# Attention forward from chunk 1 on in exponentials of 1536 columns, with two score banks of three and the background work re-timed

## The chip, the cores and the metric

One core of a Trainium2 chip runs the whole kernel: TensorE (PE) with its weight loads (PEld), VectorE (DVE), ScalarE (ACT), GpSimd (POOL), SyncE (SP, whose queue issues DMAs) and 16 DMA engines. The metric is device microseconds of one execution, the median over the runs of a kernel. PSUM, where matmuls write, has eight banks of 512 float32 columns on 128 partitions; the sizes below are counted in these banks.

## The reference

One transformer block with adaptive layer norm, forward and backward. With S = 2048 tokens, D = 512, H = 32 heads of 16, F = 1792:

```python
h = _layernorm(x) * (1 + ca) + sa
q, k, v = split_heads(h @ wqkv)
o = softmax(q @ k.T / 4) @ v
x = x + ga * (o @ wo)
h = _layernorm(x) * (1 + cb) + sb
x = x + gb * (relu(h @ w1 + b1) ** 2 @ w2 + b2)
# outputs: x, and the gradients of A_x, wqkv, wo, w1, b1, w2, b2, c, w_mod for grad_out
```

The attention of the forward pass has 32 heads x 2048 x 2048 scores, and each of them goes through one exponential on ScalarE. The backward pass computes scores and exponentials once more; the change does not touch that part.

## The kernel before, in words

Tokens are cut into four chunks of 512 queries (`SC` = 4). The forward pass runs attention chunk by chunk, and while chunk c is in attention, the matmuls of the MLP of chunk c-1, forward and backward, are slipped between its matmuls.

**Chunk 0** has its own loop in `phase_fwd` (exponential at L413), with the projections as its background. **Chunks 1 to 3** run in `fwd_rest`, which the change rewrites. Its work is 24 groups: 3 chunks x 8 groups of 4 heads. A group walks 16 key blocks of 128 keys (`kb`). One step of that loop:

- four score matmuls (L503), one per head, each on 32 rows of the PE array and 512 queries, into two tiles of two PSUM banks. The pool `fwst` has three such tiles, six banks
- two exponentials of 1024 columns on ACT (L507), PSUM to bf16 tiles `pu` in SBUF (`fwp`, six buffers)
- the "pv" matmuls of the step before (L482): for each head four matmuls of 17 columns (16 of V and a column of ones that gives the softmax sum), 16 in a step, all 4 heads x 4 query blocks of a group accumulating in 272 columns of one bank, `accbank`
- up to four matmuls of the background (`bg.burst(3.0, self, most)`), nearly all of them recorded at L158, the line of the helper `mm`
- for each of the `most` slots that the background left free, a filler matmul of 512 columns (L520) into the score tile of the next step, which the real scores overwrite later

At a group's last step DVE takes the reciprocal of the sums and multiplies (L488, L490) before `accbank` is used again; `pend` holds pv back for a step there (`held`).

The background is a queue of generators (`Background`). `burst` adds `rate` to a credit (at most 4), takes matmuls while there is credit and fewer than `most` were taken, and stops behind the last matmul of an accumulation (`k.stopped`), since the background has one PSUM bank (`mps`, one buffer) that DVE must empty first. A yielded `("wait", n)` sets `hold` to n, and each later call of `burst` then only lowers `hold`, by 2 in before, until it is no longer positive.

`gen_mlp(sc, O_b)` yields in this order: the output projection (16 matmuls), for chunk 0 the folding of bias and scales into the weights (`gen_weights_1`: 14 times four matmuls of one column, then POOL scales w1 in four pieces, L1238), a wait, the first MLP product (56 matmuls, `pps<-fT,w`), for chunk 0 `gen_weights_2`, the gradient du (56), the gradient dx (4 x 14, each followed by layer-norm backward on DVE) with `gen_do` (4 x 4) between, and the output product fc2 (4 x 15). The mark `fc2_{sc}` is yielded after `fc2(0)`; once `fc2_2` has been seen in chunk 3, the loop takes no more background, and what is left goes to `last_chunk`, which runs the MLP of chunk 3 without attention beside it: `bg.take` puts some of the left matmuls between its own, and `bg.drain` emits the rest ahead of the transposes of the normalized activations (`turn(xh[...])`, L882).

PE and SP run in the order written in the program in this phase; instructions of ACT, DVE and POOL are placed by the framework's scheduler. Waits on buffers and on data come from the framework. The rest of the kernel (weight gradients, attention backward, L1076 on) is the same in both kernels.

Of the kernel before, what the change touches and what calls it, by code (L numbers as in the profile page):

```python
# [9 lines left out]
BF16 = mybir.dt.bfloat16  # L10
F32 = mybir.dt.float32
ACT = mybir.ActivationFunctionType
ALU = mybir.AluOpType
AX = mybir.AxisListType
PSUM = bass.MemoryType.PSUM
# [4 lines left out]
P = 128  # L20
DH = 16
# [14 lines left out]
class Background:  # L36
# [41 lines left out]
    def burst(self, rate, k, most=4):  # L78

        n = 0  # L80
        if self.hold > 0:
            self.hold -= 2
            return n
        self.credit = min(self.credit + rate, 4.0)
        while self.gens and self.credit > 0 and n < most:
            k.stopped = False
            r = self.next()
            if r is None:
                break
            if isinstance(r, tuple):  # L90
                self.hold = r[1]
                break
            self.credit -= max(r, 0.25)
            n += r
            if k.stopped:
                break
        return n
# [29 lines left out]
class K:  # L127
# [164 lines left out]
    def phase_fwd(self):  # L292
# [5 lines left out]
        tc, nc, pp = self.tc, self.nc, self.pp  # L298
        S, D, H, NQ, ST, DT, FT, SC = self.S, self.D, self.H, self.NQ, self.ST, self.DT, self.FT, self.SC
# [15 lines left out]
        Vaug = fw.tile([P, ST, H, DH + 1], BF16, name="Vaug")  # L315
        kp = self.open_pool("fwk", bufs=2)
        pup = self.open_pool("fwp", bufs=6)
        self.mps = self.open_pool("mps", bufs=2, space=PSUM)
        stp = self.open_pool("fwst", bufs=2, space=PSUM)
        accp = self.open_pool("fwacc", bufs=2, space=PSUM)  # L320
        O32 = self.ra.tile([P, 4, D], F32, name="O32")
        QTm = [fw.tile([P, 512], BF16, name=f"QTm{j}") for j in range(4)]
# [16 lines left out]
        bg = Background()  # L339
        bg.add(self.gen_qkv(kp))  # L340
        pend = []
# [18 lines left out]
        KT = kp.tile([P, S], BF16, name="KTq")  # L360
# [8 lines left out]
        for n in range(2):  # L369
            accb = accp.tile([P, 512], F32, name="accbank")  # L370
            accs.append(accb[:, 0:8 * (DH + 1)].rearrange("p (a s e) -> p a s e", a=2, s=4))
        units = [(n, 4 * s + k) for s in range(SC) for n in range(2) for k in range(4)]
        for i, (n, kb) in enumerate(units):
# [4 lines left out]
            for a in range(2):  # L378
                nc.tensor.matmul(stt[:, a, :], lhsT=KT[:, kb * P:(kb + 1) * P], rhs=(QTm[2 + a] if n else QTo[a])[:],
                                 start=True, stop=True)  # L380
# [58 lines left out]
        self.fwd_rest(bg, KT, kp, pup, QTm, Vaug, O32)  # L439
        bg.until(f"fc2_{SC - 2}")  # L440
        self.OT_l = self.mk.tile([P, 4, DT, P], BF16, name="fT", bufs=2)
        self.gT_l = self.mk.tile([P, DT, 512], BF16, name="fT", bufs=2)
        nc.sync.dma_start_transpose(self.gT_l[:], self.io["grad_out"][0, S - 512:, :])
        x0s = []
        for k in range(2):
            t = self.mk.tile([P, D], BF16, name="x0", bufs=2)
# [15 lines left out]
    def fwd_rest(self, bg, KT, kp, pup, QTm, Vaug, O32):  # L462

        nc, NQ, ST, SC = self.nc, self.NQ, self.ST, self.SC
        for name in ("fwacc", "fwst", "mps"):
            self.close_pool(name)
        self.mps = self.open_pool("mps", bufs=1, space=PSUM)
        stp = self.open_pool("fwst", bufs=3, space=PSUM)
        accp = self.open_pool("fwacc", bufs=1, space=PSUM)
        groups = [(qc, g) for qc in range(1, SC) for g in range(NQ)]  # L470
        acc = None

        def pv(w):
            nonlocal acc
            ((qc, g, kb, pus), half) = w
            if kb == 0 and half == 0:
                accb = accp.tile([P, 512], F32, name="accbank")
                acc = accb[:, 0:16 * (DH + 1)].rearrange("p (a s e) -> p a s e", a=4, s=4)
            for a in range(2):
                j = 2 * half + a  # L480
                for sub in range(4):
                    nc.tensor.matmul(acc[:, j, sub, :], lhsT=pus[half][:, a, sub * P:(sub + 1) * P], rhs=Vaug[:, kb, 4 * g + j, :],  # L482
                                     start=(kb == 0 and j == 0 and sub == 0), stop=False, skip_group_check=True)
            if kb < ST - 1 or half == 0:
                return
            st0 = 4 * qc
            rl = self.rl[:, st0:st0 + 4, 4 * g:4 * g + 4].rearrange("p s a -> p a s")
            nc.vector.reciprocal(rl, acc[:, :, :, DH])  # L488
            o = O32[:, :, 4 * g * DH:4 * (g + 1) * DH].rearrange("p s (a d) -> p a s d", a=4)
            nc.vector.tensor_tensor(o, acc[:, :, :, 0:DH], rl.unsqueeze(3).to_broadcast([P, 4, 4, DH]), ALU.mult)  # L490
            if g == NQ - 1 and qc < SC - 1:
                bg.add(self.gen_mlp(qc, self.take_o(qc, O32)))

        pend = []
        tiles = None
        for n, (qc, g) in enumerate(groups):
            for kb in range(ST):
                if kb == 1 and n + 1 < len(groups):
                    KTn = self.load_group_fwd(*groups[n + 1], kp, QTm)
                tiles = tiles or [stp.tile([P, 2, 512], F32, name="st") for _ in range(2)]  # L500
                for h in range(4):
                    r = slice(32 * h, 32 * h + 32)
                    nc.tensor.matmul(tiles[h // 2][:, h % 2, :], lhsT=KT[r, kb * P:(kb + 1) * P], rhs=QTm[g % 2][r, :],  # L503
                                     start=True, stop=True)
                pus = [pup.tile([P, 2, 512], BF16, name="pu") for _ in range(2)]
                for t, pu in zip(tiles, pus):
                    nc.scalar.activation(pu[:], t[:], ACT.Exp, scale=self.scale)  # L507
                held = kb == 1 and n > 0
                while len(pend) > 1 and not held:
                    pv(pend.pop(0))  # L510
                most = 5 if held else 2 if kb == 2 and n > 0 else 4
                done = 0 if qc == SC - 1 and f"fc2_{SC - 2}" in bg.seen else bg.burst(3.0, self, most)
                if pend and not held:
                    pv(pend.pop(0))
                pend += [((qc, g, kb, pus), half) for half in range(2)]
                tiles = None
                if (n, kb) != (len(groups) - 1, ST - 1):
                    tiles = [stp.tile([P, 2, 512], F32, name="st") for _ in range(2)]
                    for _ in range(int(most - done)):
                        nc.tensor.matmul(tiles[0][:, 0, :], lhsT=KT[:, 0:P], rhs=QTm[g % 2][:], start=True, stop=True)  # L520
            KT = KTn
        while pend:
            pv(pend.pop(0))

    def gen_open(self, Vaug, KT, QTm, QTo, stp, bg):

# [695 lines left out]
    def gen_weights_1(self):  # L1222

        nc = self.nc
        D, F, DT, FT = self.D, self.F, self.DT, self.FT
        w1, wo = self.w1, self.wo
        pb = self.mps.tile([P, 1024], BF16, name="pps")
        nc.tensor.transpose(pb[:, :FT], self.b1r[:], self.ident[:FT, :FT])
        nc.vector.tensor_copy(self.b1c_b[:], pb[:, :FT])
        pt = self.mps.tile([P, 512], F32, name="pps")  # L1230
        for ft in range(FT):
            for kt in range(DT):
                self.mm(pt[:, ft:ft + 1], lhsT=w1[:, kt, ft * P:(ft + 1) * P], rhs=self.sbT_b[:, kt:kt + 1],
                                 start=(kt == 0), stop=(kt == DT - 1))
            yield 0.5
        nc.vector.tensor_tensor(self.bias1[:], pt[:, :FT], self.b1c_b[:], ALU.add)
        for kt in range(DT):
            nc.gpsimd.tensor_scalar(w1[:, kt, :], w1[:, kt, :], self.opcbT[:, kt:kt + 1], 1.0, ALU.mult, ALU.mult)  # L1238
            yield 0
        nc.sync.dma_start_transpose(self.wogaT[:].rearrange("p a b c -> p (a b) c"), wo[:].rearrange("p a b -> p (a b)"))  # L1240
# [28 lines left out]
    def gen_mlp(self, sc, O_b):  # L1269
# [33 lines left out]
        nc.gpsimd.dma_start(tm_v(self.xhat2_d), xh[:])  # L1303
        if sc == 0:
            yield from self.gen_weights_1()
            yield ("wait", 4)
        else:
            yield ("wait", 11)
        rT = self.ra.tile([P, FT * 512], BF16, name="rT")[:].rearrange("p (f k) -> p f k", f=FT)
# [18 lines left out]
            nc.vector.tensor_tensor(rT[:, ft, :], rT[:, ft, :], rT[:, ft, :], ALU.mult)  # L1328
        nc.gpsimd.dma_start(self.duT_d.rearrange("ft p s -> p ft s")[:, :, s0:s0 + 512], duT[:])
        nc.gpsimd.dma_start(self.aT_d.rearrange("ft p s -> p ft s")[:, :, s0:s0 + 512], rT[:])  # L1330
        yield ("wait", 1)
        todo = []
        for k in range(4):
# [20 lines left out]
        def fc2(k):  # L1354
            pt = mps.tile([P, 512], F32, name="pps")
            for ft in range(FT):
                self.mm(pt[:], lhsT=rT[:, ft, k * P:(k + 1) * P], rhs=self.w2[:, ft, :], start=(ft == 0), stop=False)
                yield 1
            self.mm(pt[:], lhsT=self.ones_b[0:1, :], rhs=self.b2gb_b[0:1, :], start=False, stop=True)
            yield 1  # L1360
            o = mk.tile([P, D], BF16, name="o0", bufs=2)
            nc.vector.tensor_tensor(o[:], pt[:], x1[:, k, :], ALU.add)
            nc.gpsimd.dma_start(out_v[:, k, :], o[:])

        yield from fc2(0)
        yield from self.gen_do(sc, *todo.pop(0))
        yield (f"fc2_{sc}", 0)
        for k in range(1, 4):
            yield from fc2(k)

    def ln_bwd_dve(self, wk, dxh_ps, xh, g, rstd_col, out_ap):
        nc = self.nc
# [695 lines left out]
```

## Time and profile before

| what | us |
|---|---|
| runs (median of 3) | 2517.16 (2512.57 to 2521.45) |
| the profiled execution, as timed | 2527.3 |
| its span in the trace | 2525.3 |
| chunk 0 and what comes ahead of it | 0 to about 273 |
| `fwd_rest`, first to last exponential (L507) | 275.1 to 984.3 |
| `last_chunk`, the MLP of chunk 3 | about 984 to 1062 |

The time of the profiled execution is some 10 us over the median of the runs. In the rows, "x768 | 704.9, 1127 | 6.0" is the count, then the time in which at least one instruction of the group was running, the mean duration of one in ns (neighbours overlap, so count times mean is more than the busy time), and the idle time of that engine just ahead of them. A matmul of 512 columns has a recorded duration of some 380 ns with its way through the array, while the next one starts much earlier. PEclk is the clock granted to TensorE, as a share of full speed.

### The profile page before, as it was taken

What the parts mean: (1) busy time and instruction counts of PE and PEld (TensorE: products, weight loads), DVE (VectorE), ACT (ScalarE), POOL (GpSimd) and SP (SyncE); (2) the same over time, 40 slices, a digit from 0 to 9 for tenths busy, and PEclk for the clock granted to TensorE, in tenths of its full rate; (3) what the DMA queues carried; (4) which work ended last, traced back from release to release, by engine and by line L of the source; (5) the groups of instructions that cost most, each with busy time, mean ns of one, the idle gap of its engine ahead of it and who ended that gap; (6) DMA issues with size and microseconds to landing.
All of it is one profiled execution on the core that took longest, in us unless ns stands there. A gap on an engine that the chain in (4) does not pass through costs nothing.

```text
span 2525.3 us, 69141 instructions
## 1 busy us (share of the span) xinstructions
PE 2424.0 (96%) x26994; PEld 1032.7 (41%) x27199; DVE 1683.0 (67%) x3343; ACT 2283.0 (90%) x3757; POOL 715.7 (28%) x1265
## 2 busy tenths in 40 slices
PE   8999999999999999989999999999999999999988
PEld 4555444545554544573232333332333333333333
DVE  6222212322342333576999999999999999999857
ACT  7999999999999996533999999999999999999934
POOL 2344430120121021246222332322332323222323
PEclk9999999999999999999999999999999999999999
DMA  4689650451244054599999999999999999999997
GB/s 166 133 179 209 162 124 22 127 118 48 99 103 100 22 145 120 111 188 214 236 237 226 233 237 232 236 226 228 230 233 234 233 234 234 239 227 238 241 179 188
DMA packets 1291630, 454.19 MB, mean 180 GB/s; under 512 B 1235796, under 2 KB 1260246, under 8 KB 1291302
## 3 DMA queue, kind: packets, MB, share of 16 engines
q1 hardware_dynamic: 1252422, 344.68, 72.4%
q0 software_dynamic: 36800, 104.04, 14.1%
q8 instruction: 212, 3.47, 0.6%
q10 hardware_dynamic: 2080, 1.05, 0.2%
q14 instruction: 116, 0.95, 0.1%
HBM read 75.83 MB, written 64.49 MB: 56 GB/s over the span
## 4 chain that ended last, share of the span: by engine, by line
PE 40%; ACT 8%; DMA 8%; issue 2%; DVE 2%; POOL 0%; SPq 0%; DVEq 0%; ACTq 0%; POOLq 0%
PE st L1710 16%; PE acckv L1561 8%; ACT pu L1713 6%; PE accq L1586 5%; DMA dsT<-ds 4%; PE dps L1151 2%; PE dp L1624 2%; DMA keep<-ds 1%; DMA dqT<-dq_t 1%; ACT csq L1642 1%; PE st L1856 1%; DVE ds L1628 1%; PE dp L1761 1%; PE st L1667 1%; PE st L1574 1%
## 5 line engine op out<-in xcount | busy, mean ns | idle before, releaser
L1628 DVE TENSOR_TENSOR ds<-dp,pu 128x512 bf16<-128x512 f32 x1888 | 1166.8, 684 | 36.5 <-PE dp L1624 20.6
L1713 ACT ACTIVATE pu<-st 128x512 bf16<-128x512 f32 x2048 | 1073.6, 666 | 37.2 <-PE st L1710 21.3
L507 ACT ACTIVATE pu<-st 128x1024 bf16<-128x1024 f32 x768 | 704.9, 1127 | 6.0 <-PE st L503 5.6
L1624 PE MATMUL dp<-kvm,q 64*128 64x512 bf16 x1024 | 364.0, 383 | 2.1 <-DVE ds L1628 1.0
L1624 PE MATMUL dp<-kvm,dOTg 64*128 64x512 bf16 x1024 | 364.9, 384 | 1.0 <-DVE ds L1628 0.8
L1710 PE MATMUL st<-kvm,QTg 64*128 64x512 bf16 x1024 | 348.8, 382 | 6.0
L1710 PE MATMUL st<-kvm,q 64*128 64x512 bf16 x1024 | 347.9, 381 | 5.1 <-ACT pu L1713 0.2
L1643 POOL TENSOR_TENSOR ds<-csq,pu 128x512 bf16<-128x512 f32 x128 | 147.2, 1150 | 626.5 <-ACT csq L1642 547.4
L482 PEld LDWEIGHTS <-pu 128*128 128x128 bf16 x6144 | 216.5, 96 | 158.0 <-issue 83.2
L482 PE MATMUL accbank<-Vaug,pu 128*128 128x17 bf16 x6144 | 265.2, 172 | 10.1 <-ACT pu L507 7.4
L520 PE MATMUL st<-QTm,KTq 128*128 128x512 bf16 x670 | 202.7, 379 | 6.3 <-ACT pu L507 2.7
L413 ACT ACTIVATE pu<-st 128x1024 bf16<-128x1024 f32 x224 | 206.6, 1060 | 2.3 <-PE st L410 1.9
L503 PE MATMUL st<-QTm,KTq 32*128 32x512 bf16 x1536 | 171.9, 385 | 5.2 <-issue 1.0
L1561 PE MATMUL acckv<-ds,Qg 128*16 128x512 bf16 x1024 | 176.5, 383 | 0.2
L1561 PE MATMUL acckv<-pu,dOg 128*16 128x512 bf16 x1024 | 176.4, 383 | 0.0
L1561 PE MATMUL acckv<-ds,q 128*16 128x512 bf16 x1024 | 175.8, 382 | 0.0
L1561 PE MATMUL acckv<-pu,q 128*16 128x512 bf16 x1024 | 175.8, 382 | 0.0
L410 PE MATMUL st<-QTm,KTq 128*128 128x512 bf16 x435 | 130.0, 377 | 10.1 <-ACT pu L413 4.0
L1710 PEld LDWEIGHTS <-q 64*128 64x128 bf16 x1024 | 66.9, 94 | 162.9 <-issue 150.0
L1710 PEld LDWEIGHTS <-QTg 64*128 64x128 bf16 x1024 | 67.1, 94 | 161.5 <-issue 146.5
L347 PEld LDWEIGHTS <-pu 128*128 128x128 bf16 x2048 | 86.4, 96 | 59.6 <-issue 3.0
L1624 PEld LDWEIGHTS <-q 64*128 64x128 bf16 x1024 | 88.8, 93 | 51.3 <-issue 40.8
(399 smaller groups left out, 3365.7 us busy)
## 6 DMA issues: line engine op xcount, KB each, us to landing
KTq<-KTq_d POOLq DMA_DIRECT2D x24, 512.0 KB, 3.8
duT_d<-auT POOLq DMA_DIRECT2D x3, 1792.0 KB, 7.3
aT_d<-rT POOLq DMA_DIRECT2D x3, 1792.0 KB, 11.9
KTq_d<-KTq SPq DMA_DIRECT2D x32, 128.0 KB, 2.2
QTq_d<-ev_fm SPq DMA_DIRECT2D x32, 128.0 KB, 4.4
ktm_d<-ev_tm POOLq DMA_DIRECT2D x32, 128.0 KB, 2.6
VTq_d<-vT POOLq DMA_DIRECT2D x4, 1024.0 KB, 6.1
dx<-dx_d SPq DMA_DIRECT2D x16, 256.0 KB, 4.6
```

The source lines that it names most:

```text
L410: nc.tensor.matmul(stt[:, a, :], lhsT=KT[:, kb * P:(kb + 1) * P], rhs=QTm[2 * jp + a][:], start=True, stop=True)
L413: nc.scalar.activation(pu[:], stt[:], ACT.Exp, scale=self.scale)
L482: nc.tensor.matmul(acc[:, j, sub, :], lhsT=pus[half][:, a, sub * P:(sub + 1) * P], rhs=Vaug[:, kb, 4 * g + j, :], start=(kb == 0 and j == ...
L503: nc.tensor.matmul(tiles[h // 2][:, h % 2, :], lhsT=KT[r, kb * P:(kb + 1) * P], rhs=QTm[g % 2][r, :], start=True, stop=True)
L507: nc.scalar.activation(pu[:], t[:], ACT.Exp, scale=self.scale)
L520: nc.tensor.matmul(tiles[0][:, 0, :], lhsT=KT[:, 0:P], rhs=QTm[g % 2][:], start=True, stop=True)
L1561: nc.tensor.matmul(acckv[r:r + DH, :], lhsT=T[n][:, ib, col:col + DH], rhs=src[:, a, :], start=(ib == 0), stop=(ib == ST - 1))
L1624: nc.tensor.matmul(dp[:], lhsT=T["dOT"][rd, ib * P:(ib + 1) * P], rhs=masked["VT"][a][rd, 512 * c:512 * (c + 1)], start=True, stop=True)
L1628: nc.vector.tensor_tensor(dsg[:, i, a], dp[:], pu[:, a, :], ALU.mult)
L1643: nc.gpsimd.tensor_tensor(dsg[:, i, 1], f[:], pu[:, 1, :], ALU.mult)
L1710: nc.tensor.matmul(stt[:], lhsT=T["QT"][rs, q], rhs=masked["KT"][a][rs, c0:c0 + 512], start=True, stop=True)
L1713: nc.scalar.activation(pu[:, a, :], stt[:], ACT.Exp, scale=self.scale)
```

## The change

- `fwd_rest` no longer goes by key blocks with four heads but by **units of three score tiles**: the 24 x 16 x 4 = 1536 tiles (group, key block, head) are cut into 512 units of three. A unit has three score matmuls into one tile of three banks (`fwst`: two tiles of three banks in place of three of two) and one exponential of 1536 columns. `pu` has four buffers of 1536 columns; `fwp` is closed and opened anew for that.
- pv works per tile (four matmuls of 17 columns): `outputs` takes up to six tiles that are at least two units old; the first call in a unit, ahead of the scores, only where a group's last tile is among them. Behind a group's end it holds the next group's tiles for one or two units.
- The background gets at most `int((1.32 - spent) / 0.215)` matmuls in a unit and a rate of 2.5, where `spent` is 0.33 for the scores and 0.1 for each pv tile. `hold` falls by 1.4 in a call.
- Fillers: while an accumulator is open, matmuls of 240 columns into the unused columns 272 to 511 of `accbank`; between accumulators, the unit's own scores repeated.
- `gen_weights_1` waits (2) ahead of its matmuls and yields 1 for each four; the wait behind it goes from 4 to 10.
- The turned grad_out of chunk 3 (`gT_l`, a transposing DMA on SP's queue) is asked for inside the MLP of chunk 2, ahead of dx, in place of after the loop.
- The mark `fc2_{sc}` comes after `fc2(1)` in place of `fc2(0)`.

```diff
@@ burst
-            self.hold -= 2
+            self.hold -= 1.4
@@ phase_fwd
         self.OT_l = self.mk.tile([P, 4, DT, P], BF16, name="fT", bufs=2)
-        self.gT_l = self.mk.tile([P, DT, 512], BF16, name="fT", bufs=2)
-        nc.sync.dma_start_transpose(self.gT_l[:], self.io["grad_out"][0, S - 512:, :])
@@ fwd_rest
-        stp = self.open_pool("fwst", bufs=3, space=PSUM)
+        stp = self.open_pool("fwst", bufs=2, space=PSUM)
         accp = self.open_pool("fwacc", bufs=1, space=PSUM)
+        pup = self.open_pool("fwp", bufs=4)
...
+        tiles = [(n, kb, h) for n in range(len(groups)) for kb in range(ST) for h in range(4)]
+        units = [tiles[i:i + 3] for i in range(0, len(tiles), 3)]
+        pend, ready = [], 0
+
+        def outputs(u, last_of):
+            nonlocal ready
+            n = 0
+            while n < 6 and pend and pend[0][0] <= u - 2 and not (accb is None and u < ready):
+                if last_of and not any(t[1:] == (ST - 1, 3) for (v, t, _) in pend if v <= u - 2):
+                    break
+                (_, t, p) = pend.pop(0)
+                n += 1
+                if pv(*t, p):
+                    ready = u + (1 if bg.hold > 0 or not bg.gens else 2)
+            return n
+
+        for u in range(len(units) + 2):
+            spent = 0.1 * outputs(u, True)
+            if u < len(units):
+                st = stp.tile([P, 3, 512], F32, name="st")
+
+                def scores():
+                    for i, (n, kb, h) in enumerate(units[u]):
+                        r = slice(32 * h, 32 * h + 32)
+                        nc.tensor.matmul(st[:, i, :], lhsT=KTs[n][r, kb * P:(kb + 1) * P], rhs=QTm[n % 2][r, :],
+                                         start=True, stop=True)
+
+                for (n, kb, h) in units[u]:
+                    if (kb, h) == (1, 0) and n + 1 < len(groups):
+                        KTs[n + 1] = self.load_group_fwd(*groups[n + 1], kp, QTm)
+                scores()
+                spent += 0.33
+            spent += 0.1 * outputs(u, False)
+            if u >= len(units):
+                continue
+            if groups[n][0] < SC - 1 or f"fc2_{SC - 2}" not in bg.seen:
+                spent += 0.215 * bg.burst(2.5, self, int((1.32 - spent) / 0.215))
+            if accb is not None:
+                for _ in range(int((1.2 - spent) / 0.1)):
+                    nc.tensor.matmul(accb[:, W:512], lhsT=KTs[n][:, 0:P], rhs=QTm[n % 2][:, W:512], start=False, stop=False,
+                                     skip_group_check=True)
+            else:
+                for _ in range(int((1.1 - spent) / 0.33)):
+                    scores()
+            pu = pup.tile([P, 3, 512], BF16, name="pu")
+            nc.scalar.activation(pu[:], st[:], ACT.Exp, scale=self.scale)
+            pend += [(u, t, pu[:, i, :]) for i, t in enumerate(units[u])]
@@ gen_weights_1
+        yield ("wait", 2)
...
-            yield 0.5
+            yield 1
@@ gen_mlp
-            yield ("wait", 4)
+            yield ("wait", 10)
...
+        if sc == SC - 2:
+            self.gT_l = mk.tile([P, DT, 512], BF16, name="fT", bufs=2)
+            nc.sync.dma_start_transpose(self.gT_l[:], io["grad_out"][0, self.S - 512:, :])
         yield ("wait", 1)
...
         yield from self.gen_do(sc, *todo.pop(0))
+        yield from fc2(1)
         yield (f"fc2_{sc}", 0)
-        for k in range(1, 4):
-            yield from fc2(k)
+        yield from fc2(2)
+        yield from fc2(3)
```

More of the change, by code (lines that the diff above doesn't have):

```diff
@@ L464, in fwd_rest, with pv @@
         nc, NQ, ST, SC = self.nc, self.NQ, self.ST, self.SC
-        for name in ("fwacc", "fwst", "mps"):
+        for name in ("fwacc", "fwst", "mps", "fwp"):
             self.close_pool(name)
         self.mps = self.open_pool("mps", bufs=1, space=PSUM)
-        stp = self.open_pool("fwst", bufs=3, space=PSUM)
+        stp = self.open_pool("fwst", bufs=2, space=PSUM)
         accp = self.open_pool("fwacc", bufs=1, space=PSUM)
+        pup = self.open_pool("fwp", bufs=4)
         groups = [(qc, g) for qc in range(1, SC) for g in range(NQ)]
[L471 to L476, printed above, removed]
-                accb = accp.tile([P, 512], F32, name="accbank")
[L478 to L485, printed above, removed]
+        W = 16 * (DH + 1)
+        KTs = {0: KT}
+        accb = None
+        def pv(n, kb, h, p):
+            nonlocal accb
+            qc, g = groups[n]
+            if (kb, h) == (0, 0):
+                accb = accp.tile([P, 512], F32, name="accbank")
+            acc = accb[:, 0:W].rearrange("p (a s e) -> p a s e", a=4, s=4)
+            for sub in range(4):
+                nc.tensor.matmul(acc[:, h, sub, :], lhsT=p[:, sub * P:(sub + 1) * P], rhs=Vaug[:, kb, 4 * g + h, :],
+                                 start=(kb == 0 and h == 0 and sub == 0), stop=False, skip_group_check=True)
+            if (kb, h) != (ST - 1, 3):
+                return False
             st0 = 4 * qc
@@ L490, in pv @@
             nc.vector.tensor_tensor(o, acc[:, :, :, 0:DH], rl.unsqueeze(3).to_broadcast([P, 4, 4, DH]), ALU.mult)
+            accb = None
             if g == NQ - 1 and qc < SC - 1:
                 bg.add(self.gen_mlp(qc, self.take_o(qc, O32)))
[L494 to L521, printed above, removed]
@@ L522, in fwd_rest @@
-        while pend:
-            pv(pend.pop(0))
+            return True
+        tiles = [(n, kb, h) for n in range(len(groups)) for kb in range(ST) for h in range(4)]
[12 more added lines that the diff above has]
+            return n
```

## The prediction

> **What bounds the kernel now.** I read the page's slices first, then the groups, then the stage of the change by itself.
>
> ```profile
> span 2525.3 us, 69141 instructions
> ...
> PE   8999999999999999989999999999999999999988
> ...
> ACT  7999999999999996533999999999999999999934
> ...
> L507 ACT ACTIVATE pu<-st 128x1024 bf16<-128x1024 f32 x768 | 704.9, 1127 | 6.0 <-PE st L503 5.6
> ```
>
> ```profile
> 275.00:984.30 709.30, 683.38 (x9096) 352.01 (x9227) 213.74 (x516) 704.95 (x768) 127.00 (x187) 1.00 0.38 94
> ```
>
> The second fence is the table of stretches for the stage (length, then PE, PEld, DVE, ACT and POOL busy, granted clock). Both PE and ACT look full, but ACT is busy 704.95 of 709.30 us with one kind of instruction and waits 6.0 us in all, while PE's share holds fillers. So ACT bounds the stage: 768 exponentials, end to end. Their price per column and per instruction comes from the views of the two lines of exponentials (min/median/max ns) and a long run in the timeline:
>
> ```profile
> L507 ACT ACTIVATE pu<-st x768: 1018/1110/1379, 275.1 to 983.1; 128x1024 bf16<-128x1024 f32 x192
> ```
> ```profile
> L1713 ACT ACTIVATE pu<-st x2048: 592/658/827, 1179.8 to 2391.6; 128x512 bf16<-128x512 f32 x187
> ```
> ```profile
> 898.37 46.95 ACT L507 ACTIVATE pu<-st 128x1024 bf16<-128x1024 f32 x51
> ```
>
> The shortest of 1024 and of 512 columns differ by 426 ns for 512 columns: 0.832 ns a column. Fifty-one in a row took 46.95 us; with the last one's own 1.02 taken off, fifty steps of 0.918 us. Of these 0.852 are columns, so about 0.066 us is paid once per instruction.
>
> **The change, part by part.**
>
> *Wider exponentials.* 512 instructions of 1.278 + 0.066 = 1.344 us are 688.1 us, against 768 x 0.918 = 705.0: **-16.9 us**. The columns stay the same; only 256 fixed prices go. No row shows 1536 columns, so the bounds: the fixed price might grow with the banks read (then 1.5 x 0.918 = 1.377 a unit, gain 0), and at most the whole gap of the shortest instruction, 1.018 - 0.852 = 0.166 us, could go 256 times, 42 us. I take 0.066, since it comes from the row of this very loop. The Trainium skill, "ScalarE: Activation LUTs", section "What ACT_TABLE_LOAD costs", gives 0.833 ns a column, 186 ns an instruction (93 more for a pointer operand) and an overlap of 93 between neighbours, so 93 ns at least would be saved each time and the first term would be -23.8. The slope agrees with the rows; a fixed price of 93 would make 768 steps 726 us, more than the stage has, so the rows decide.
>
> *Does PE keep up with 1.344 us a unit?* Five rows of one step give its prices:
>
> ```profile
> 641.25 0.81 PE L520 MATMUL st<-QTm,KTq 128*128 128x512 bf16 x3
> 641.99 0.40 PE L503 MATMUL st<-QTm,KTq 32*128 32x512 bf16 x4
> 642.32 0.36 PE L482 MATMUL accbank<-Vaug,pu 128*128 128x17 bf16 x8
> 642.53 1.02 PE L158 MATMUL pps<-fT,W2gbT 128*128 128x512 bf16 x4
> 643.39 0.35 PE L482 MATMUL accbank<-Vaug,pu 128*128 128x17 bf16 x8
> 643.68 0.50 PE L503 MATMUL st<-QTm,KTq 32*128 32x512 bf16 x4
> ```
>
> From start to start: four scores 0.33 (they run side by side on their rows, so three cost the same), eight pv matmuls 0.21 (0.105 per tile of four), a background matmul 0.215, and the turn from a full matmul to scores 0.74 - 3 x 0.215 = 0.095. A 240-column filler is not in the trace. It stands between one of 128 columns and one of 512:
>
> ```profile
> 1060.13 0.83 PE L1096 MATMUL dps<-tm_blk,xh 128*128 128x128 bf16 x12
> 1060.80 0.39 PE L1096 MATMUL dps<-tm_l,xh 128*128 128x128 bf16 x4
> ```
>
> Twelve of 128 columns take 0.67, 0.056 each; 0.026 (17 columns), 0.056 and 0.215 lie nearly on a line, which gives 0.10 at 240. A unit with three tiles of pv and three background matmuls is 0.33 + 0.095 + 0.315 + 0.645 = 1.385, a bit over ACT's 1.344; with one, 1.26 with its fillers; without any, 1.24. Walking the generators' yields through the new rule gives 764 background matmuls, 1040 fillers, 36 rounds of repeated scores in 26 units, and 170 units of the 1.385 kind. Sum: 512 x 0.425 + 1536 x 0.105 + 764 x 0.215 + 1040 x 0.10 + 36 x 0.33 = 659 us, 1.287 a unit. The credit of 2.5 a unit allows four or five of the long units in a row, 0.2 us of delay, and the scores may be late: they can start when ACT leaves their tile and must be in PSUM one exponential later, 1.344 - 0.40 = 0.94 us of play. So ACT stays the bound, with the third score tile gone, but PE's reserve is only 4%. With the filler at its ends, 0.056 and 0.215, the sum is 613 to 779, and at the upper one PE would bind at 1.52 a unit; the straight line through three rows excludes that for me, but each 0.01 on it is worth 10 us of PE, and 29 us are all the reserve.
>
> *The same walk shows when the background ends.* For before it puts the mark of chunk 2 at step 372 of 384, 12 x 1.836 = 22 us before the end; the trace's last background matmuls of the stage stand at
>
> ```profile
> 959.92 0.59 PE L158 MATMUL pps<-wogaT,dxT 128*128 128x512 bf16 x2
> ```
>
> 24 us before 984.3. For after it gives unit 472 of 512: 54 us before the end, so the longer waits and the extra fc2 are hidden by attention. Without that cover every matmul would cost 0.215 at the end.
>
> *The longer wait behind `gen_weights_1`.*
>
> ```profile
> 338.03 6.96 POOL L1238 TENSOR_SCALAR w<-w,opcbT 128x1792 bf16<-128x1792 bf16 x4
> ```
> ```profile
> 343.31 0.39 PE L158 MATMUL pps<-fT,w 128*128 128x512 bf16 x1 [0.80 <-POOL w L1238]
> 345.05 0.39 PE L158 MATMUL pps<-fT,w 128*128 128x512 bf16 x1 [1.34 <-POOL w L1238]
> ```
> ```profile
> 346.05 1.94 ACT L507 ACTIVATE pu<-st 128x1024 bf16<-128x1024 f32 x2 [2.23 <-PE st L503]
> 349.00 1.94 ACT L507 ACTIVATE pu<-st 128x1024 bf16<-128x1024 f32 x2 [1.01 <-PE st L503]
> ```
>
> In before the background's first MLP matmuls came while POOL still scaled w1, and PE, in order, held the next scores: ACT stood still 2.23 and 1.01 us. The new wait skips 8 units, 10.7 us, in place of 2 steps, 3.7: the matmuls come 7 us later than at 341.9, when POOL is done (345.0). **-3.2 us.** Bounds: 0 if POOL starts later, too.
>
> *fc2(1) moves into attention.* In `last_chunk` one accumulation less is drained ahead of the transposes:
>
> ```profile
> 997.69 3.18 PE L158 MATMUL pps<-w,rT 128*128 128x512 bf16 x14 [1.27 <-DVE o L1362]
> 1000.80 0.39 PE L158 MATMUL pps<-b2gb_b,ones_b 1*128 1x512 bf16 x1
> 1001.97 3.18 PE L158 MATMUL pps<-w,rT 128*128 128x512 bf16 x14 [0.78 <-DVE o L1362]
> 1005.08 0.38 PE L158 MATMUL pps<-b2gb_b,ones_b 1*128 1x512 bf16 x1
> 1005.40 0.62 PE L882 MATMUL tp<-ident,xh 128*128 128x128 bf16 x8
> ```
> ```profile
> 999.34 0.81 ACT L924 ACTIVATE xh<-x_l,nmr,rstd 128x512 bf16<-128x512 f32 x1 [1.46 <-DVE nmr L923]
> ```
>
> What the transposes need is done at 1000.15, so nothing else is late until then, and the second block falls out with its wait: 0.78 + 3.43 = **-4.2 us**. Bounds: 0 (a later DMA could take over) and 5.2, the way down to 1000.15.
>
> *The turned grad_out.* Asked for earlier, it only moves:
>
> ```profile
> 965.14 2.98 SPq L443 DMA_TRANSPOSE fT<-in_grad_out_dram  x1
> ```
> ```profile
> 993.13 1.03 PE L911 MATMUL dps<-fT,W2gbT 128*128 128x512 bf16 x4
> ```
>
> It was 25 us early already; ahead of dx it holds SP's queue 2.98 us, and the first dx transposes are asked for a whole 14-matmul accumulation later. 0, at worst 3.
>
> *New waits.* At each of 24 group ends the next pv waits for DVE to empty `accbank`, and scores, background and fillers stand behind it on PE; the rule holds pv one or two units, 1.34 us or more, against 0.26 + 0.42 of DVE (L488 and L490 in their groups) and perhaps one 0.69 ahead of them. Where scores are repeated, the exponential waits for the last repeat: about 1.2 of 1.344 us. I take 0.1 per group end, **+2.5 us**, between 0 and 0.9 each.
>
> Sum: -16.9 - 3.2 - 4.2 + 2.5 = -21.8. On the profiled execution (2527.3, some 10 over the median of the runs) that is 2505.5; on the median, 2517.2 - 21.8 = **2495 us**.
>
> **Rivals.**
>
> *The stage doesn't get shorter* (chance 0.18): PE binds at 1.377 a unit, which takes only 0.09 more per unit than my sum (a restart after each wait for a score tile), or ACT's fixed price grows with the banks. For it: a reserve of 4%, and two tiles in place of three. Against it: the sum already has the turns, and PE in before ran 93% (0.33 + 0.095 + 0.42 + 0.86 of 1.836) by the same prices without holding ACT. Then -3.2 - 4.2 + 2.5 = -4.9: 2512.
>
> *The clock falls* (0.06), slower than before. Drops stand in the trace where PE was thin:
>
> ```profile
> 342.81:346.22 3.41, 1.56 (x22) 0.85 (x23) 0.74 (x1) 1.18 (x3) 2.18 (x2) 1.00 1.45 233
> 346.22:349.63 3.41, 3.37 (x31) 1.36 (x30) 0.01 (x1) 2.40 (x3) 0.00 (x0) 0.50 0.94 211
> ...
> 640.00:660.00 20.00, 19.52 (x257) 10.19 (x262) 7.87 (x21) 20.00 (x24) 0.78 (x2) 1.00 0.01 2
> ```
>
> PE busy 1.56 of 3.41 us, and the next 3.41 ran at 0.50, which cost ACT 1.01 us. The place here is the group ends with repeated scores and the small wait in each unit. Twenty-two drops eat the gain, from thirty on the kernel is slower by over 0.3%; with one in four of the stage's 200 stretches of 3.41 us, 50 drops, it is -22 + 50 = +28: 2545. Against it: even a unit of three rounds of scores keeps PE busy for 1.0 of 1.344 us, far over 1.56 of 3.41. By the Trainium skill, "TensorE: Matmul & The Clock Gate", section "A second HAM failure mode: psum-queue depth-cycling", a PE that idles briefly between groups while cycling PSUM banks swings between half and full clock, which speaks against this change; the row at 640 shows the like of it, small waits in each step at 1.00.
>
> **How the numbers follow.** The forecast has 0.70, its own range 2489 to 2504 (terms at 0 one by one, or the group ends free). The first rival 0.18, the second 0.06, and 0.06 for what I don't see, mostly 0 to +10. The range 2487 to 2513 takes in the forecast's own and the first rival's 2512; the clock, a dearer filler and half of what I don't see stay outside. A measurement tells 0.3%, 7.5 us, from no change: faster 0.74 (the forecast and some of the rest), same 0.17, slower 0.09.
>
> **What would show it.** In after: 512 exponentials, a median step of 1.34 us and ACT busy over 98% of a stage of about 690 us; no POOL release of PE near the first MLP matmuls; one fc2 block between the last xh and its transposes; the clock at 1.00. I am wrong if steps of 1.38 or more appear with "PE st" as the releaser, if the clock row shows 0.50 at group ends, or if DVE releases pv for long.

## The result, and the profile after

The changed kernel takes 2502.9 us, median of 18 runs (2493.7 to 2515.8); the kernel before, run beside it, 2521.3 (2508.4 to 2528.4; its three runs of the table above were among them). The ratio is 0.9934, with a 95% interval of 0.9917 to 0.9951: 16.6 us less, or 12 to 21 (the two medians differ by 18.3). The profiled execution of after took 2499.4.

The page, the table of stretches for the new stage (length, PE, PEld, DVE, ACT, POOL busy, granted clock, DMA) and the view of the exponentials' line answer to the first rows of the prediction:

```profile
span 2497.7 us, 69518 instructions
...
PE   8999999999999999999999999999999999999998
...
ACT  7999999999999997535999999999999999999934
...
L540 ACT ACTIVATE pu<-st 128x1536 bf16<-128x1536 f32 x512 | 690.3, 1614 | 10.2 <-PE st L519 10.0
```
```profile
274.00:972.30 698.30, 676.67 (x9570) 363.95 (x9620) 212.02 (x517) 690.32 (x512) 129.16 (x189) 0.98 0.37 96
```
```profile
L540 ACT ACTIVATE pu<-st x512: 1444/1594/2035, 274.0 to 970.4; 128x1536 bf16<-128x1536 f32 x171
```
```profile
628.45 114.28 ACT L540 ACTIVATE pu<-st 128x1536 bf16<-128x1536 f32 x85
```

The last row is a long run of exponentials without a stop: 85 in 114.28 us; with 1.444 taken off for the last one, 84 steps of 1.343 us. That is the step that 0.832 ns a column and 0.066 an instruction give. But ACT now waits 10.2 us, 10.0 of them for PE, in place of 6.0 and 5.6, and the clock of the stage is 0.98 in place of 1.00.

Where the time went, from the two traces (us; a step goes from the end of one exponential to the end of the next, an undisturbed step is the mean of those that are not late, and "excess" is what all steps have over it, summed):

| | before | after | difference |
|---|---|---|---|
| first to last exponential of the stage | 709.0 | 698.3 | -10.7 |
| of it: undisturbed steps | 704.0 (768 x 0.9166) | 687.7 (512 x 1.3432) | -16.3 |
| of it: excess | 4.9 | 10.5 | +5.6 |
| last exponential to the transposes of xh | 21.3 | 15.9 | -5.4 |
| the exponentials of attention backward, first to last | 1212.4 | 1206.8 | -5.6 |

The last line is code that the change does not touch. In the kernels below, with the same code there, it took 1208.4 to 1220.0 us; so it and the rest of the 27.6 us between the two spans belong to the executions, and the change's own part is the 10.7 + 5.4 = 16.1 us of the lines above, near the 16.6 of the runs.

The excess of after has three sources, each with its rows. First, the clock. The stretch ahead of each of two falls and the one or three behind it at half clock, and last a stretch that no fall followed:

```profile
448.73:452.14 3.41, 2.71 (x49) 1.45 (x49) 0.19 (x1) 3.41 (x4) 1.76 (x2) 1.00 0.69 277
452.14:455.55 3.41, 3.41 (x30) 1.05 (x27) 0.00 (x0) 3.31 (x3) 0.00 (x0) 0.50 1.01 375
...
769.59:773.00 3.41, 2.42 (x44) 1.15 (x38) 2.22 (x8) 3.41 (x4) 1.57 (x2) 1.00 0.48 179
773.00:783.24 10.24, 10.24 (x106) 5.10 (x105) 0.87 (x2) 8.41 (x6) 0.81 (x1) 0.50 0.44 104
...
943.67:947.08 3.41, 2.42 (x31) 0.87 (x28) 0.68 (x2) 3.41 (x4) 0.00 (x0) 1.00 0.00 0
```

PE was busy 2.71 of 3.41 us, and the clock still went to 0.50. PE then ran without a pause and could not keep up. The busy time does not tell which stretch is followed by a fall: 2.42 us were followed by one at 773 us and by none at 947. What stands ahead of the drops at 452 and 773 us is a group end at which the background holds; here the PE timeline (start, length, instruction, count, idle time before it):

```profile
770.31 0.83 PE L519 MATMUL st<-QTm,KTq 32*128 32x512 bf16 x9 [0.44 <-ACT pu L540]
771.66 0.39 PE L519 MATMUL st<-QTm,KTq 32*128 32x512 bf16 x3 [0.52 <-ACT pu L540]
```

Three rounds of scores end after 0.83 us, as the rule counts 0.33 for a round where 0.22 pass, and PE stands still for 0.52 of the 1.34 us. Second, one stop at `accbank`:

```profile
564.73 0.26 DVE L487 RECIPROCAL rl<-accbank 128x16 f32<-128x16 f32 x1
565.85 1.91 DVE L1319 TENSOR_SCALAR xh<-x,mv,rstd 128x512 bf16<-128x512 f32 x4 [0.85 <-POOL rstd L1316]
567.68 0.42 DVE L489 TENSOR_TENSOR O<-accbank,rl 128x256 f32<-128x256 f32 x1
```
```profile
568.15 0.70 PE L481 MATMUL accbank<-Vaug,pu 128*128 128x17 bf16 x20 [1.99 <-DVE O L489]
```

DVE's order puts the normalization of the MLP, which waits for POOL, between the two instructions that empty the bank. PE waited 1.99 us and ACT 1.70, and the clock fell for 6.8 us. Third, ends of groups where a repeated round comes late and ACT waits for it. By steps: 6.2 us belong to half-clock stretches (1.2 at the stage's start, 0.8, 1.6 and 2.6 at 452, 570 and 776 us), 1.8 to the stop at `accbank`, 2.4 to the other group ends.

### The profile page after: what moved, and what is told of

The parts are those of the page before. It is cut to its first block, busy times and chain, and to the rows that moved or that the text cites. A ratio compares the mean times of both kernels' runs of the same rounds, so it can differ in the third digit from the quotient of the medians.

```text
span 2497.7 us, 69518 instructions
## 1 busy us (share of the span) xinstructions
PE 2410.6 (97%) x27474; PEld 1042.3 (42%) x27601; DVE 1681.5 (67%) x3343; ACT 2267.5 (91%) x3501; POOL 717.0 (29%) x1265
## 3 DMA queue, kind: packets, MB, share of 16 engines
q0 software_dynamic: 36800, 104.04, 13.7%
## 4 chain that ended last, share of the span: by engine, by line
PE 42%; ACT 8%; DMA 6%; issue 2%; DVE 2%; POOL 1%; SPq 0%; DVEq 0%; ACTq 0%; POOLq 0%
PE st L1733 17%; PE acckv L1584 8%; ACT pu L1736 6%; PE accq L1609 5%; DMA dsT<-ds 4%; PE dps L1169 2%; PE dp L1647 2%; PE dp L1784 1%; PE st L1879 1%; DMA keep<-ds 1%; ACT csq L1665 1%; DVE ds L1651 1%; PE st L1597 1%; PE st L1690 1%; DMA out_dram<-dw 1%
## 5 line engine op out<-in xcount | busy, mean ns | idle before, releaser
L1736 ACT ACTIVATE pu<-st 128x512 bf16<-128x512 f32 x2048 | 1072.0, 661 | 32.9 <-PE st L1733 21.3
L540 ACT ACTIVATE pu<-st 128x1536 bf16<-128x1536 f32 x512 | 690.3, 1614 | 10.2 <-PE st L519 10.0
L481 PEld LDWEIGHTS <-pu 128*128 128x128 bf16 x6144 | 187.6, 96 | 118.2 <-issue 108.4
L481 PE MATMUL accbank<-Vaug,pu 128*128 128x17 bf16 x6144 | 233.6, 172 | 3.0 <-DVE O L489 2.0
L519 PE MATMUL st<-QTm,KTq 32*128 32x512 bf16 x1632 | 211.9, 388 | 14.8 <-ACT pu L540 8.8
L413 ACT ACTIVATE pu<-st 128x1024 bf16<-128x1024 f32 x224 | 206.5, 1059 | 1.0 <-PE st L410 0.7
L534 PE MATMUL accbank<-QTm,KTq 128*128 128x240 bf16 x1066 | 159.3, 271 | 1.1 <-issue 0.2
L410 PE MATMUL st<-QTm,KTq 128*128 128x512 bf16 x435 | 129.9, 377 | 9.0 <-ACT pu L413 4.0
L1733 PEld LDWEIGHTS <-q 64*128 64x128 bf16 x1024 | 67.0, 94 | 163.0 <-issue 149.8
L519 PEld LDWEIGHTS <-KTq 32*128 32x128 bf16 x1632 | 65.2, 91 | 163.6 <-issue 158.7
L347 PEld LDWEIGHTS <-pu 128*128 128x128 bf16 x2048 | 86.4, 96 | 59.1 <-issue 2.3
```

Of the source, the lines that this page charges most:

```text
L413: nc.scalar.activation(pu[:], stt[:], ACT.Exp, scale=self.scale)
L481: nc.tensor.matmul(acc[:, h, sub, :], lhsT=p[:, sub * P:(sub + 1) * P], rhs=Vaug[:, kb, 4 * g + h, :], start=(kb == 0 and h == 0 and sub = ...
L519: nc.tensor.matmul(st[:, i, :], lhsT=KTs[n][r, kb * P:(kb + 1) * P], rhs=QTm[n % 2][r, :], start=True, stop=True)
L534: nc.tensor.matmul(accb[:, W:512], lhsT=KTs[n][:, 0:P], rhs=QTm[n % 2][:, W:512], start=False, stop=False, skip_group_check=True)
L540: nc.scalar.activation(pu[:], st[:], ACT.Exp, scale=self.scale)
L1733: nc.tensor.matmul(stt[:], lhsT=T["QT"][rs, q], rhs=masked["KT"][a][rs, c0:c0 + 512], start=True, stop=True)
```

## The experiments

**e1: the wait behind `gen_weights_1`.**

```diff
-            yield ("wait", 10)
+            yield ("wait", 4)
```

> The changed kernel with the wait behind gen_weights_1 back at 4 (three units skipped in place of eight). Theory (the longer wait removed before's stop of 3.4 us at about 346 us): the first MLP matmuls of the background come some 6.7 us earlier, while POOL still scales w1; PE is released by POOL L1256 or its like two or three times, the exponentials stop for 2 to 3.5 us there, and the granted clock may fall to 0.50 just behind. Rival (the narrower pace of 1.34 us a unit already delays the matmuls enough, the wait does nothing): no release by POOL, no exponential step over 1.5 us between 330 and 360 us.

The timelines of PE and ACT:

```profile
339.74 0.61 PE L158 MATMUL pps<-fT,w 128*128 128x512 bf16 x1 [2.50 <-POOL w L1257]
341.47 0.61 PE L158 MATMUL pps<-fT,w 128*128 128x512 bf16 x1 [1.12 <-POOL w L1257]
```
```profile
342.73 1.45 ACT L540 ACTIVATE pu<-st 128x1536 bf16<-128x1536 f32 x1 [4.24 <-PE st L519]
345.06 1.45 ACT L540 ACTIVATE pu<-st 128x1536 bf16<-128x1536 f32 x1 [0.88 <-PE st L519]
```

The stop is back, and larger than before's: 4.24 + 0.88 + 0.80 us, with 10.2 us at half clock in it. With the wait of 10 no step over 1.44 us stands between 307 and 450 us. The stage as a whole (696.8) is no longer than after's, since the drops at 452, 568 and 773 us did not occur in this run, though one at 945 did; the stage of one profile can't measure such an edit, only its own place can.

**e2: the mark ahead of fc2(1).**

```diff
-        yield from fc2(1)
         yield (f"fc2_{sc}", 0)
+        yield from fc2(1)
```

> The changed kernel with the mark fc2 back ahead of fc2(1). Theory: last_chunk has two drained fc2 blocks between the last xh and the transposes of xh again, and the distance from the last exponential of the stage to the first of these transposes grows by 4.2 us (4.0 to 4.5); the stage before it is the same within what clock drops make of it. Rival (something else would end last there, a DMA or DVE): under 2 us.

```profile
989.52 0.38 PE L158 MATMUL pps<-b2gb_b,ones_b 1*128 1x512 bf16 x1
990.68 3.18 PE L158 MATMUL pps<-w,rT 128*128 128x512 bf16 x14 [0.78 <-DVE o L1384]
993.80 0.38 PE L158 MATMUL pps<-b2gb_b,ones_b 1*128 1x512 bf16 x1
994.12 0.62 PE L900 MATMUL tp<-ident,xh 128*128 128x128 bf16 x8
```

The second block is back, 0.78 + 3.44 us to the transposes. The distance from the last exponential is 21.4 us in place of 15.9: 5.5, of which about 1.2 goes with a half-clock stretch that began at 973.2 (before had one at 984.5, after none there). In e3 below, with one block and such a stretch at 972.2, the distance is 17.2. The block's price is the 4.2 of the forecast.

**e3: repeated rounds counted at 0.215.**

```diff
-                for _ in range(int((1.1 - spent) / 0.33)):
+                for _ in range(int((1.1 - spent) / 0.215)):
                     scores()
```

> The changed kernel with the repeated rounds of scores counted at 0.215 us, which is what the trace shows for one (nine matmuls in 0.83), in place of 0.33: one or two rounds more in the units between two accumulators. Theory (the clock falls at group ends because PE idles 0.3 to 0.5 us in two or three units in a row): drops that follow a group end without a wait for DVE (at about 452 and 773 us in after) are gone, at most one or two stretches of 0.50 in the stage besides the one at its start, the exponentials' excess over their step falls from 10.5 us to 5 to 8, the stage from 698.3 to about 694. Rival (the drops come from somewhere else, or the rounds make ACT wait): as many drops as in after (three places besides the start), or steps of 1.38 us and more in the 26 units with repeated rounds, stage 698 or longer.

The drops at 452 and 773 us are gone; the one behind the stop at `accbank` (569.4) and the one at the stage's start remain, the latter for 10.2 us. Excess 9.0, stage 696.9, where 5 to 8 and 694 were expected. The smaller gain comes from what the rival named:

```profile
306.96 0.86 PE L519 MATMUL st<-QTm,KTq 32*128 32x512 bf16 x9
```
```profile
307.67 1.45 ACT L540 ACTIVATE pu<-st 128x1536 bf16<-128x1536 f32 x1 [0.29 <-PE st L519]
```

Behind a background matmul the three rounds end too late, and ACT waits 0.29 us. That the drops at 452 and 773 us are gone would not show the cause by itself, as e1 has neither of them and the rounds of after. All the runs together do: the four kernels with rounds counted at 0.215 (e3, e7, e9, e11) have no half clock in the stage but at its start and behind the stop at `accbank`, and the six other kernels with the new loop and its fillers have one to three drops elsewhere in it. So the rounds hold the clock, and they stand in ACT's way.

**e4: the old loop with the two small edits** (wait 12, mark behind fc2(1); attention as before).

> The kernel before with two of the small edits alone: the wait behind gen_weights_1 at 12 (six steps, 11 us) and the mark behind fc2(1). Attention loop, exponentials of 1024 columns and fillers as before. Theory: the stop at about 346 us is gone, stage 709.0 to about 705.5; last_chunk 4.2 us shorter from the last exponential to the transposes of xh; in all -7.6 us, with no change of the exponentials' step of 0.917. Rival (these edits need the new pace, and all the gain is the wider exponentials'): stage within 1 us of 709, last_chunk within 1 us.

Stage 706.7, excess 2.6 in place of 4.9; no step of the exponentials between 333 and 352 us is late (21 in 19.58 us). Last exponential to the transposes 15.8. The two parts gain 2.3 + 5.5 us, some 1.2 of the latter since the half clock that before has at 984.5 us is missing.

**e5: without the fillers.**

```diff
-                for _ in range(int((1.2 - spent) / 0.1)):
+                for _ in range(0):
```

> The changed kernel without the 1040 matmuls of 240 columns into accbank (the repeated scores stay); the result is unchanged. Theory (the clock follows how much PE does, and only the background's long units suffer from a drop): the granted clock stands at 0.50 in most stretches where the background holds, 100 us or more of the stage, and each time the background comes back its first one or two units take about 1.97 us in place of 1.34; with some 20 to 30 such places the stage gets 15 to 40 us longer than 698. Rival (the fillers only cost PE time, the clock holds without them): PEclk over the stage at 0.95 or more, stage 690 to 698.

The table of stretches, the whole stage and one part:

```profile
274.00:1019.20 745.20, 666.79 (x8559) 310.31 (x8554) 211.51 (x518) 698.45 (x512) 127.62 (x188) 0.76 0.34 89
561.00:585.00 24.00, 21.59 (x239) 8.85 (x238) 5.34 (x10) 20.95 (x16) 2.69 (x5) 0.50 0.08 24
```

Less work on PE makes the stage 46.9 us longer, more than the 15 to 40 expected: 363 us of it are at half clock, against 27 in after. That is 98 stretches of 3.41 us more, 0.48 us each on average, less than the 0.8 in after. In the second row PE is at half clock throughout, and ACT is still busy for 20.95 of 24.00 us. The first part of after's excess hangs on the clock, and the fillers hold it.

**e6: `accbank` emptied at high priority on DVE.**

```diff
-            nc.vector.reciprocal(rl, acc[:, :, :, DH])
             o = O32[:, :, 4 * g * DH:4 * (g + 1) * DH].rearrange("p s (a d) -> p a s d", a=4)
-            nc.vector.tensor_tensor(o, acc[:, :, :, 0:DH], rl.unsqueeze(3).to_broadcast([P, 4, 4, DH]), ALU.mult)
+            with self.tc.high_priority():
+                nc.vector.reciprocal(rl, acc[:, :, :, DH])
+                nc.vector.tensor_tensor(o, acc[:, :, :, 0:DH], rl.unsqueeze(3).to_broadcast([P, 4, 4, DH]), ALU.mult)
```

> The changed kernel with the reciprocal and the multiplication that empty accbank given high priority on DVE, so that no normalization of xh stands between them. Theory: the stop at about 570 us (3155 and three steps of 1973 ns, 3.4 us in all) is gone with the two half-clock stretches behind it, and PE no longer waits for DVE O L489; stage 698.3 to about 695. Rival (DVE, in order, now stands waiting for PE in front of other work and empties the background's bank late): PE waits for the background's evictions (DVE auT, DVE rT, DVE o) rise above 2 us in all, stage 699 or longer.

```profile
565.21 0.26 DVE L489 RECIPROCAL rl<-accbank 128x16 f32<-128x16 f32 x1
566.32 0.55 DVE L1320 TENSOR_SCALAR xh<-x,mv,rstd 128x512 bf16<-128x512 f32 x1 [0.85 <-POOL rstd L1317]
566.78 0.42 DVE L490 TENSOR_TENSOR O<-accbank,rl 128x256 f32<-128x256 f32 x1
567.12 1.45 DVE L1320 TENSOR_SCALAR xh<-x,mv,rstd 128x512 bf16<-128x512 f32 x3
```

One normalization still slips in, but three no longer do: PE waits 0.6 us for L490, and the late step at 570 us is 1.86 in place of 3.16. PE's waits for other evictions stay at 1.0 us in all. Stage 693.7, excess 5.8. Of the 4.6 us that the stage is shorter, 2.4 are at this place. Another 2.6 are the drop at 773 us, which did not occur; it is missing in e1 and e2 too, which leave DVE's order as it is, so it is not shown to be the edit's doing.

**e7: two held units, and rounds counted at 0.215 up to 1.0.**

```diff
-                    ready = u + (1 if bg.hold > 0 or not bg.gens else 2)
+                    ready = u + 2
...
-                for _ in range(int((1.1 - spent) / 0.33)):
+                for _ in range(int((1.0 - spent) / 0.215)):
```

> The changed kernel with two edits: behind every group end the next group's pv waits two units (in before one, where the background holds), and repeated rounds are counted at 0.215 us up to 1.0 us in place of 0.33 up to 1.1. Theory: the stop at 570 us shrinks from 1.8 us to under 0.7, the added rounds keep the clock and end early enough not to hold ACT; excess over the exponentials' step 5 to 7 us in place of 10.5, stage about 693 to 695. Rival (two units without pv leave PE thin however the rounds are counted): more half-clock stretches than in after (27 us), stage over 699.

Stage 694.6, excess 6.7, half clock 13.7 us in the stage; the stop is 0.3 us, but the drop behind it, at 568 us, is still there with three slow steps.

**e8: the turned grad_out behind the loop again.**

> The changed kernel with the turned grad_out asked for behind the loop, as before. Theory (it was hidden anyway): the distance from the last exponential to the transposes of xh stays within 0.5 us of 15.9 us (1.2 more if a half-clock stretch falls there), no matmul of the first du product waits for a DMA. Rival (the earlier request is needed since the loop's end now comes with less background behind it): du waits for the DMA fT, 1 to 5 us.

15.9 us to the transposes as in after, and no du matmul waits. It was hidden. The stage's 700.3 has one more drop than after, at 396 us, over the same instructions.

**e9, e10, e11, e12.** e9 joins e6's priority with e7's count of rounds, e11 adds e7's held units to that, e10 is e4's kernel again and e12 is e6's, over 12 and 6 runs.

> The changed kernel with accbank emptied at high priority (as in e6) and repeated rounds counted at 0.215 us up to 1.0 (as in e7). Theory: both causes of the lost time are mended, so the half-clock stretches in the stage are those at its start and one or two more, excess 4 to 6 us, stage 692.5 to 694; against before 24 us less (0.990), 5 us better than the changed kernel's 0.9934. Rival (the drops are a matter of where the stretches fall, and mending one place opens another): excess 8 us or more, ratio 0.993.

> The kernel of e4 (before's loop with the longer wait and the later mark), timed. Theory: 6.5 to 8 us under before, ratio 0.9970 to 0.9975, so that of the change's 18 us some 7 are these two edits and some 11 the wider exponentials less the clock drops. Rival: ratio 0.999 or more, all gain from the exponentials.

> The kernel of e9 with two units held behind every group end as in e7. Theory: with accbank emptied in time a second held unit has nothing left to gain; it makes PE thinner there, so stage and excess are the same as in e9 within 1 us, or up to 2 us more. Rival (PE still waits for accbank in e9): excess 1 us or more under e9's and PE's waits for DVE O at 0.

> The kernel of e6 (only the emptying of accbank at high priority), timed. Theory: stage 693.7 against 698.3, so some 4.6 us under the changed kernel: ratio to before about 0.9915 (0.9905 to 0.9925), the same as e9's within its interval, since the counted rounds of e9 bought nothing more. Rival (e6's one time was a lucky one): ratio 0.9930 or more, the stage back at 697 or longer in the new profile.

| | ratio to before (95% interval) | stage | excess | half clock (whole stretches that touch the stage) |
|---|---|---|---|---|
| after | 0.9934 (0.9917 to 0.9951) | 698.3 | 10.5 | 27.3 |
| e9 | 0.9910 (0.9882 to 0.9939) | 694.2 | 6.4 | 13.7 |
| e10 | 0.9958 (0.9940 to 0.9977) | 707.5 | 3.4 | 3.4 |
| e11 | one run, 2494.7 us | 694.6 | 6.7 | 13.7 |
| e12 | 0.9909 (0.9880 to 0.9939) | 704.0 | 16.2 | 61.4 |

e10: the two small edits alone are worth 10.6 us by the runs (6 to 15) and 7.0 by its trace. That leaves some 6 of the change's 16.6 us for the new loop; the stages say 8 to 9 (706.7 and 707.5 against 698.3), but the intervals of after and e10 overlap, so the runs by themselves do not show it. e11 gains nothing over e9. e9 and e12 lie 6 us under after by their ratios, but the intervals overlap, so neither is shown to be better. The single execution of e6 had taken 2485.4 us; the six of e12 take 2491.9 to 2517.6, so that time was a lucky one. The new profile of e12, the same kernel as e6, has a stage 10.3 us longer, nearly all of it from one place:

```profile
314.10:351.60 37.50, 37.50 (x463) 18.74 (x461) 2.77 (x7) 31.41 (x23) 19.42 (x17) 0.50 0.63 130
```
```profile
321.57 1.45 ACT L541 ACTIVATE pu<-st 128x1536 bf16<-128x1536 f32 x1 [0.23 <-PE st L520]
323.25 1.45 ACT L541 ACTIVATE pu<-st 128x1536 bf16<-128x1536 f32 x1 [0.23 <-PE st L520]
```

Steps of 1.68 us in a row while PE is never idle. Most of it is where `gen_weights_1` runs, whose four one-column matmuls the change counts as one of 0.215 us, so that a unit has three fillers in place of five; in e6 the same instructions ran at full clock. More fillers there were not tried.

Over the runs the same is seen: the mean granted clock of an execution is 0.9952 in the 17 runs of before beside e9 and 0.9892 in the 18 of after, from 0.982 (2515.8 us) to 0.992 (2493.7 to 2499.4).

## Why the prediction was right, and where its sizes were off

The bound held: ACT's steps in the stage are 1.343 us against a forecast of 1.344, and PE's prices were right too, but for the repeated round of scores (0.22 us, not 0.33). After's long unit takes 1.38 us from scores to scores (1.385 forecast), and the filler that no row showed 0.10. By the forecast the wider exponentials were worth 16.9 us; the steps show 16.3. ACT's fixed price does not grow with the banks read, so that rival falls, and so does PE as the bound at full clock.

The stop behind `gen_weights_1` was sized at 3.2 us; the excess it made in before was 3.6, and e1 brings it back. fc2(1) was 4.2, and e2 shows 4.2. The turned grad_out was 0, and e8 shows 0. The background ended 39 us ahead of attention (its last matmul starts at 933.15, in unit 484), not the 54 of the count (unit 472); the longer waits and fc2(1) were hidden all the same.

What failed is the term of new waits, +2.5 us. Before's excess without its stop is 1.3 us, after's 10.5: the term is +9.2. Of its own mechanism, group ends, it had the size right but for one place: 2.4 us, and 1.8 more of one stop at `accbank`, twice its bound of 0.9 for a group end, which had allowed for one normalization ahead of the drain and not for four that wait for POOL. The 6.2 us of half clock it did not hold. It stood in the prediction apart from the sum, as a rival with a chance of 0.06, argued away by "even a unit of three rounds of scores keeps PE busy for 1.0 of 1.344 us, far over 1.56 of 3.41". That was the wrong step twice: three rounds take 0.83, since the step counted a round at the 0.33 of one that a pv matmul follows; and the busy share is not the edge, as the clock fell after 2.71 of 3.41 and held after 2.42. The rival's place was right, its count wrong (8 stretches in the stage, not 50), and its price per stretch, 1.0 us, near: 0.8 to 2.6 us for one to three in a row. By the Trainium skill, "TensorE: Matmul & The Clock Gate", section "A second HAM failure mode: psum-queue depth-cycling", a PE that idles briefly and often between groups of matmuls lets the clock swing; after's rows at 452 and 773 us agree, and the row at 640 in before did not. How much hangs on the clock here, e5 shows.

So the sum by terms is -16.3 - 3.6 - 4.2 + 9.2 = -14.9, another 1.2 are the drop at 984.5 that after's profile lacks, and the runs say -16.6 where -21.8 was forecast. More than half of what the wider exponentials bring, 9.2 of 16.3 us, is lost again, most of it at half clock.

Of the signs by which the prediction would call itself wrong, all three did show in places: ACT waits for "PE st" behind steps over 1.38 us, the clock row has 0.50 at group ends, and DVE held pv for 1.99 us. The time stayed in its range because these places are few. That they are few is in part luck: the same instructions ran 37.5 us at half clock in e12 and none of it in e6.

## What to carry to other kernels

On an engine that bounds a stage, an instruction's fixed price times the instructions saved is the gain to forecast (16.9 us here, 16.3 measured), and a shortest duration at two widths with one long run gives it before the change is made. What the faster pace costs elsewhere has to be priced with the same care; here it was over half of that gain. Where another engine's clock follows its work, fillers are part of the schedule: count them at the duration that the trace shows for each place, and keep them out of what the bounding engine waits for. A drain of an accumulator is two instructions or more on an in-order engine, and what the scheduler puts between them is a wait of everything behind the bank.

## What the runs showed of the hardware

A granted clock of 0.50 can hold although TensorE is never idle: 37.50 us busy of 37.50 in e12, eleven stretches of 3.41 us; 10.24 of 10.24 in after. The Trainium skill, "TensorE: Matmul & The Clock Gate", section "What's actually happening", has the throttle released by a busy window of about 3.4 us of sustained activity; these rows do not agree with busy time as that activity. All these stretches have many matmuls of 17 columns and scores on 32 rows each. No experiment tried whether work counts rather than time, but an estimate from the 14 traces speaks for it. Take a matmul's work as its columns times the share of the 128 rows that it uses, at 0.42 ns a column (0.215 us for 512), and sum it over the 3.41 us stretches of the stage. In the 41 stretches at full clock that a fall followed it is 0.16 to 0.37 of the stretch; of the 2626 that none followed, all but three have more than 0.375. At half clock, 119 stretches that half clock followed have 0.39 or less, and 55 that full clock followed have 0.36 to 0.44. Nine scores in a unit of 1.344 us come to 0.36, and e12's unit of 1.68 us to 0.33. Outside the stage 18 of 61 falls came behind more than 0.40, so this is not the whole rule.

An exponential's step is 0.832 to 0.833 ns a column plus 0.063 to 0.066 us at 1024 and at 1536 columns: three PSUM banks read by one instruction cost no more per column than two.
